# A front that mixes projections with maxima: four copy buffers, six weight-part buffers, rows grouped at the end of the queries, a key row of its own

## The chip, the core and the metric

The kernel runs on one core of a Trainium2 chip. The metric is the device time of one execution in microseconds (us), lower is better. The engines are named as the profile names them: PE (TensorE, matrix multiply), ACT (ScalarE), DVE (VectorE), POOL (GpSimd) and SP (SyncE, which here only issues DMAs). Every engine works through its own list of instructions in order and waits for the others by semaphores; a DMA queue does the same.

## The reference

Two kinds of attention read the same 2048 x 512 input `x`, and a gate mixes them row by row:

```python
x = A_x                                             # 1 x 2048 x 512
g = _sigmoid((x * gate_w).sum(-1, keepdims=True))
a = _A_ref(x, A_wqkv, A_wo)   # 32 heads of 16: each row attends to itself and 7 rows before it, 2 apart
b = _B_ref(x, B_wq, B_wk, B_wv, B_wo)   # 32 query heads, one key head and one value head, full softmax over 2048 rows
return g * a + (1 - g) * b
```

`_A_ref` projects `x @ wqkv` to 1536 columns, `_B_ref` projects 512 columns of queries, 16 of keys and 16 of values. All data are f32. The kernel splits a factor into a high part in the short f32r format and a low part (the rest), and makes a product from three matmuls: high by high, high by low, low by high.

## The kernel before, in words

**Order.** Nothing is scheduled by a tool. The Python code writes the instructions in the order in which it runs, and it decides that order with its own small clock (`clk["pe"]`, `clk["act"]`, `clk["dve"]`, `pool`): whenever a matmul is due, it asks whether a bank is free by that clock, and whether some other piece of work fits beside it. The engines then follow this order, whatever their real times are. Deferred steps lie in a list `tasks` with a due time; `settle(kind, n)` writes out all tasks of a kind but the last `n`.

**Stages.** First a short start (keys, values, first two queries). Then the *front*, `front_stream`: it works through `lumps`, called row parts here: 14 query parts `("q", m)`, then 48 parts `("a", gg, j)` of the projection for branch A, which come in three groups `gg` of 16 (each group is 512 of the 1536 columns, each `j` is 128 rows). Each row part is 12 matmuls on the upper half of the array's rows and 12 on the lower half, and the two halves (two *lines*, `b` = 0 and 1) run side by side. After the front comes the main stage, 512 steps of scores, exponentials and weighted sums for branch B, with POOL working on branch A meanwhile.

**Fours.** The lines take the row parts in fours: line 0 in the order 1st, 3rd, 2nd, 4th and line 1 in the order 2nd, 4th, 1st, 3rd. A row part is thus begun by one line and ended by the other, in the same PSUM bank. The line that comes second may begin only when `may` knows that the first has ended there. There are 62 row parts, so the fourth four holds two query parts and two parts of `gg` 0, and the last group has two row parts.

**Fills.** Between the matmuls of the row parts stand *fills*: scores whose maxima over the keys branch B needs before its exponentials. Early fills are plain: a matmul (line 382) and a DVE maximum (420, 432). Later ones work on halves: max(a, b) = (a+b)/2 + |a-b|/2, where a matmul (481) gives the difference, ACT takes its absolute value (511), another matmul (481) the half sum, and DVE adds both and reduces (529). The half keys come from a matrix `sel`, which `half_sel` builds on DVE from `whole_k` (443 to 449). `whole_k` lies in a buffer with the tag `wkl`, in which every third `qhi` tile (high part of a query, written out by DMA at line 264) lies too.

**Copies of row parts.** When a row part of branch A is done, `a_post` copies its bank to a tile `stage` in SBUF (ACT, line 315) and puts off a task `store`, which writes it by two or three DMAs on SP's queue to `ad` in DRAM (309), in pieces of up to 96 f32 numbers (384 bytes). `stage` has two buffers, so a copy waits until the store of the copy before the last has landed. On ACT everything behind the copy waits too.

**Weights of branch A.** A group has four weight chunks `c` of 128 rows. POOL's queue loads one (`load_wa`, 168) into one of two `waraw` buffers, ACT makes the high part (`split_wa`, recorded at line 119), and POOL makes the low part `wal` a little later (179, a task of the kind `low`). `wah` and `wal` have `WB` buffers each; the first twelve tiles in them are raw parts of `x`. `ahead_wa` loads the next group's chunks at `j` = 2, 4, 6, 8 and splits them at `j` = 5, 7, 9, 11, as many as there are buffers for. Row part `j` uses chunk `c` in its matmuls `i` = 3c to 3c+2, and `may` holds a line back until the low part has been written into the program.

**POOL.** `run_pool` hands POOL the next pieces of branch A while POOL is less than 2.5 us ahead by the kernel's clock; it is not called in the last two row parts of groups 0 and 1.

Of the kernel before, what the change touches and what calls it, by code (L numbers as in the profile page):

```python
# [6 lines left out]
F32 = mybir.dt.float32  # L7
# [6 lines left out]
P = 128  # L14
# [3 lines left out]
DH = 16  # L18
NJ = S // P
C = D // P  # L20
# [13 lines left out]
GG = 3  # L34
GN = NAG * AN // GG
# [9 lines left out]
LEAD, M2S, M1S, E1S, PER_ROW = 3.0, 0.5, 0.3, 0.2, 21  # L45
M2H = 0.15
JUST = 0.05
WB = 8


T_R, T_LAT, T_EXP, T_RED2, T_RED1, T_W, T_TTR = 0.23, 0.20, 0.92, 1.14, 0.61, 1.21, 0.70
# [34 lines left out]
def gated_mix_kernel(ctx, tc, xt, wa, wk, wq, wo_a, wo_b, out):  # L86
# [3 lines left out]
    wp = ctx.enter_context(tc.tile_pool(name="work", bufs=2))  # L90
# [42 lines left out]
    p1 = tc.alloc_tile_pool(name="phase1", bufs=1)  # L133
    p0 = tc.alloc_tile_pool(name="phase0", bufs=1, side="right")
# [7 lines left out]
    wkl = p0.tile([P, C, P], F32R, name="wkl")  # L142
    wqr = [p1.tile([P, 2, C, P], F32, name="wqr", tag="dd", bufs=2) for _ in range(2)]
    waraw, wah, wal = {}, {}, {}

    first = wp.tile([P, 4, 512], F32, name="xraw", tag="aext", bufs=2)
# [23 lines left out]
    def split_wa(gg, c):  # L170
        hi = wah[gg, c] = p1.tile([P, GN], F32R, name="wah", bufs=WB)
        raw = waraw.pop((gg, c))
        high(hi, raw)
        at = after("act", clk["pe"], 0.62)

        def rest():
            nonlocal pool
            wal[gg, c] = p1.tile([P, GN], F32R, name="wal", bufs=WB)
            nc.gpsimd.tensor_sub(wal[gg, c], raw, hi.bitcast(F32))
            pool = max(pool, clk["pe"] * 1e3) + 1300  # L180

        tasks.append((at + 0.3, rest, (), "low"))

    def ahead_wa(gg, k):

        if 0 <= k < 2 * C and k % 2 == 0:
            load_wa(gg, k // 2)
        if 2 < k <= (2 * C if gg == 0 else 2 * (WB - C)) + 1 and k % 2:
            split_wa(gg, (k - 3) // 2)
# [120 lines left out]

    def a_post(gg, j, bank):

        settle("store", 1)
        own = p1.tile([P, GN], F32, name="stage", bufs=2)
        nc.scalar.activation(own, bank, AF.Copy)  # L315
        at = after("act", clk["pe"] + T_LAT, 0.52)

        def store():
            for piece in a_pieces(gg):
                a_store(own, gg, j, *piece)  # L320

        tasks.append((at + 0.5, store, (), "store"))
        if j == NJ - 1:
            tasks.append((at + 1.0, whole, (gg,)))
# [59 lines left out]
    issued, seen, known = [0], {}, [-1]  # L384
# [27 lines left out]
    def fill_pair(dst, key):  # L412
        if dst is m2:
            dst = m2.whole()
        v, pr, t, kc = slots.pop(0)
        m = unit_tile(v)
        mark("m20", "m21")
        for odd in range(2):
            max_mm(dst[:, odd, :], v, pr, t, kc, odd)
        nc.vector.tensor_reduce(m[:, :, pr, t, kc], dst, AX.X, ALU.max)  # L420
        free[key] = after("dve", after("pe", 0, T_R) + T_LAT, T_RED2) + 0.08
        filled(v, 2)
# [16 lines left out]

    def half_sel():  # L440

        whole_k = p0.tile([P, 2, DH], F32, name="wholek", tag="wkl", bufs=1)
        nc.vector.tensor_add(whole_k, twin[:, :, 0, :, 0], twin[:, :, 0, :, 1])
        sel.append(p0.tile([P, 2, P], F32R, name="sel", tag="wkh", bufs=1))
        dd.extend(p1.tile([P, 2, 512], F32, name="dd", bufs=2) for _ in range(2))
        for x in range(2):
            to = sel[0][:, x].rearrange("p (b h z) -> p b h z", b=2, h=2)
            nc.vector.tensor_scalar(to[:, :, 0].rearrange("p b (d s) -> p b d s", s=2), whole_k.unsqueeze(3).to_broadcast([P, 2, DH, 2]), 0.5 - x, 0.0, op0=ALU.mult, op1=ALU.add)
            nc.vector.tensor_scalar(to[:, :, 1].rearrange("p b (s d) -> p b s d", s=2), whole_k.unsqueeze(2).to_broadcast([P, 2, 2, DH]), 0.5 - x, 0.0, op0=ALU.mult, op1=ALU.add)
        after("dve", 0, 1.0)  # L450
# [580 lines left out]
    lumps = []  # L1031
# [18 lines left out]
    def settle(kind, n):  # L1050
        for task in [t for t in tasks if t[3:] == (kind,)][:-n or None]:
            tasks.remove(task)
            task[1](*task[2])
# [141 lines left out]
    def mm(b, at):  # L1195
        nonlocal pool
        x, i = at
        lump = lumps[x]
        if x not in items:
            if lump == ("q", 9):  # L1200
                half_sel()
            elif lump == ("q", 10):
                wants.extend((1, 0))
            items[x] = queries(lump[1]) if lump[0] == "q" else a_project(*lump[1:])
            clk["pe"] = max(clk["pe"], free[f"f{x % 4}"])
            mark(f"f{x % 4}")
        l, r = items[x][i]
        if type(r) is tuple:
            r = r[0][r[1:]]
        h = slice(64 * b, 64 * b + 64)  # L1210
        second = b != x % 2
        nc.tensor.matmul(front_bank(x), l[h], r[h], start=(not second and i == 0), stop=(second and i == 3 * C - 1))  # L1212
        if i == 3 * C - 1:
            ends_at[x] = seen[f"f{x % 4}"] = issued[0]
        issued[0] += 1
        return T_R

    ends_at, posted = {}, set(range(-4, 0))

    def front_bank(x):  # L1220
        return eb[(1, 1, 0, 0)[x % 4]][:, x % 2, :]
# [1 line left out]
    def may(b, x, i):  # L1223
        lump = lumps[x]
        if lump[0] == "a" and (lump[1], i // 3) not in wal:
            return False
        return i > 0 or (x - 4 in posted if b == x % 2 else x in ends_at and known[0] >= ends_at[x])

    def front_stream():

        n, many = 3 * C, len(lumps)
        lines = [[], []]
        for x in range(0, many, 4):
            four = list(range(x, min(x + 4, many)))
            lines[0] += four[0::2] + four[1::2]
            lines[1] += four[1::2] + four[0::2]
        lines = [[(x, i) for x in line for i in range(n)] for line in lines]
        at, idle, begun = [0, 0], 0, False
        while min(at) < n * many:
            lone = {}  # L1240
            if wants and free["m2"] <= clk["pe"] + 0.1:
                half_keys(wants.pop(0))
            halves = groups or any(pend) or paired() and not (half or ended or wants) and free["m2"] <= clk["pe"] + 0.3
            if halves:
                for b in range(2):
                    if sum_ready(b):
                        lone[b] = lambda b=b: fill_sum(b)
                    elif diff_ready(b):
                        lone[b] = lambda b=b: fill_diff(b)
                        break  # L1250
            else:
                for dst, key in ((m1, "m1"), (po, "po")):
                    if not lone and fillable() and free[key] <= clk["pe"] - just():
                        lone[half[0][4] if half else 0] = lambda dst=dst, key=key: fill_one(dst, key)
            moved = []
            for b in sorted((0, 1), key=lambda b: b not in lone):
                if b in lone:
                    now = clk["pe"]
                    lone[b]()
                    clk["pe"] = now  # L1260
                elif at[b] < n * many and may(b, *lines[b][at[b]]):
                    mm(b, lines[b][at[b]])
                    moved.append(lines[b][at[b]])
                    at[b] += 1
            if lone or moved:
                idle = 0
                after("pe", 0, T_R)
            else:
                idle += 1
                assert idle < 400  # L1270
                clk["pe"] += 0.05
                run_tasks()
            if not (ended or wants or halves or formed) and slots and fillable() and free["m2"] <= clk["pe"] - just():
                clk["pe"] = max(clk["pe"], free["m2"])
                fill_pair(m2, "m2")
            if min(at) >= n * many - 9:
                ended.add(1)
            if min(at) >= n * many - 7 and not begun:
                begun = True
                eb[0] = ebs[0].whole()  # L1280
                free["e0"] = max(free["f2"], free["f3"])
                exp_pair(0, 0)
            for x, i in moved:
                if i == n - 1 and counted.count(x):
                    lump_done(x)
                elif i == n - 1:
                    counted.append(x)
            if moved and moved[-1][1] % 3 == 2:
                run_tasks()
                lump = lumps[min(x for x, i in moved)]  # L1290
                if p2 and not (lump[0] == "a" and lump[1] + 1 < GG and lump[2] > NJ - 3):
                    run_pool()
# [61 lines left out]
    for s in range(NS + 1):  # L1354
# [17 lines left out]
        k, n = (outs + rows) // 4 - 1, C - (outs >= NJ - 4)  # L1372
# [19 lines left out]
        first = 0  # L1392
# [3 lines left out]
        while order:  # L1396
            which = order.pop(0)
            if which == "later":
                order[:0] = ["m1", 1] if free["e1"] > clk["pe"] - E1S or bare[0] and free["m1"] < clk["pe"] - 1.0 else [1, "m1"]
                first = 0  # L1400
            elif which == "m2":
                fill_ready("m2", M2S)
            elif which == "m1":
                one = not later_rows and (kt or not s or u >= NU - 8) and singles(s)
                bare[0] = not one
                if one:
                    first = half[0][4] if half else 0
# [95 lines left out]
```

## Time and profile before

| | |
|---|---|
| median of 3 runs | 1464.08 us (1461.46 to 1466.11) |
| the profiled execution, its own time | 1462.15 us |
| its span, first to last instruction | 1460.4 us |
| PE busy | 1435.4 us (98%) |
| ACT / DVE / POOL busy | 1295.5 / 1153.5 / 966.5 us |
| front, first to last matmul of line 1212 | 24.0 to 295 us |

The span is what the trace covers. A window row gives, for a stretch of the span, the busy time of each engine with its number of instructions (x), then the granted PE clock (1.00 is full), the busy share of the DMA engines and the GB/s. A waits row says which engine and line waited for whom: total, times, longest. In a timeline row the bracket at the end is the idle time of that engine just before the instruction, and what ended it.

### The profile page before, as it was taken

What the parts mean: (1) busy time and instruction counts of PE and PEld (TensorE: products, weight loads), DVE (VectorE), ACT (ScalarE), POOL (GpSimd) and SP (SyncE); (2) the same over time, 40 slices, a digit from 0 to 9 for tenths busy, and PEclk for the clock granted to TensorE, in tenths of its full rate; (3) what the DMA queues carried; (4) which work ended last, traced back from release to release, by engine and by line L of the source; (5) the groups of instructions that cost most, each with busy time, mean ns of one, the idle gap of its engine ahead of it and who ended that gap; (6) DMA issues with size and microseconds to landing.
All of it is one profiled execution on the core that took longest, in us unless ns stands there. A gap on an engine that the chain in (4) does not pass through costs nothing.

```text
span 1460.4 us, 29278 instructions
## 1 busy us (share of the span) xinstructions
PE 1435.4 (98%) x10524; PEld 672.6 (46%) x10524; DVE 1153.5 (79%) x1882; ACT 1295.5 (89%) x1645; POOL 966.5 (66%) x1749
## 2 busy tenths in 40 slices
PE   9898999999999999999999999999999999999998
PEld 7676666633333333333333367433333336433343
DVE  8776878878887888888888889788888888788712
ACT  5597878799999999999999988999999998899986
POOL 5451486788898988888889888979888805111121
PEclk9999999999999999999999999999999999999999
DMA  6553433222120210112323110221202010000110
GB/s 226 168 158 99 133 81 115 75 80 63 41 86 14 84 33 30 60 28 75 99 51 98 46 56 31 86 64 44 67 22 72 12 40 28 16 1 2 30 30 30
DMA packets 106970, 94.03 MB, mean 64 GB/s; under 512 B 84880, under 2 KB 89016, under 8 KB 102728
## 3 DMA queue, kind: packets, MB, share of 16 engines
q1 hardware_dynamic: 99864, 52.95, 13.4%
q0 software_dynamic: 6240, 37.89, 7.9%
q8 instruction: 83, 1.36, 0.4%
q10 hardware_dynamic: 720, 1.31, 0.3%
q14 instruction: 63, 0.52, 0.1%
HBM read 62.13 MB, written 29.45 MB: 63 GB/s over the span
## 4 chain that ended last, share of the span: by engine, by line
PE 90%; DMA 2%; issue 2%; ACT 2%; POOL 2%; DVE 2%; SPq 0%; ACTq 0%; POOLq 0%; DVEq 0%
PE po L584 34%; PE pe L574 23%; PE pe L1212 8%; PE pm L382 8%; PE ps L382 5%; PE pe L889 4%; PE pm L481 4%; PE ps L481 2%; PE po L481 1%; DMA ad<-stage 1%; PE pm L943 1%; POOL qst L208 1%; DVE mx L420 1%; ACT dd L511 1%; ACT pexp L576 0%
## 5 line engine op out<-in xcount | busy, mean ns | idle before, releaser
L576 ACT ACTIVATE pexp<-pe 128x1024 f32<-128x1024 f32 x1022 | 983.7, 1023 | 63.9 <-PE pe L574 60.9
L420 DVE TENSOR_REDUCE mx<-pm 128x2 f32<-128x1024 f32 x487 | 595.8, 1223 | 169.1 <-PE pm L382 157.7
L584 PE MATMUL po<-pexp,vst 128*32 128x512 f32 x4096 | 545.5, 605 | 0.4 <-ACT pexp L576 0.4
L574 PE MATMUL pe<-qst,kst 64*128 64x512 f32 x1788 | 419.7, 454 | 1.9 <-ACT pexp L576 1.2
L574 PEld LDWEIGHTS pe<-qst,kst 64*128 64x128 f32 x1788 | 167.5, 183 | 443.5 <-ACT pexp L576 435.7
L432 DVE TENSOR_REDUCE mx<-ps 128x1 f32<-128x512 f32 x309 | 210.3, 681 | 1.7 <-PE ps L382 1.5
L648 POOL TENSOR_TENSOR pr<-aext 128x256 f32<-128x256 f32 x256 | 182.4, 741 | 5.5 <-DMA aext<-ad 5.2
L382 PE MATMUL pm<-kst,qst 62*128 62x512 f32 x913 | 183.4, 397 | 0.4
L711 POOL TENSOR_TENSOR oa<-oa,av 128x256 f32<-128x256 f32 x224 | 164.4, 734 | 15.9
L511 ACT ACTIVATE dd<-pm 128x512 f32<-128x512 f32 x252 | 145.9, 600 | 25.3 <-PE pm L481 6.6
L584 PEld LDWEIGHTS po<-pexp,vst 128*32 128x32 f32 x4096 | 80.6, 108 | 147.1 <-issue 137.0
L708 POOL TENSOR_TENSOR av<-aext,lg 128x256 f32<-128x256 f32 x224 | 139.6, 623 | 12.8
L1212 PE MATMUL pe<-wah,xh 64*128 64x512 f32 x384 | 132.9, 399 | 4.2 <-ACT stage L315 4.2
L1212 PE MATMUL pe<-wal,xh 64*128 64x512 f32 x384 | 131.6, 399 | 0.0
L1212 PE MATMUL pe<-wah,xl 64*128 64x512 f32 x384 | 130.7, 396 | 0.0
L481 PE MATMUL pm<-kcd,qst 62*128 62x512 f32 x286 | 112.7, 404 | 5.6 <-ACT dd L511 5.3
L382 PE MATMUL ps<-kst,qst 62*128 62x512 f32 x291 | 114.8, 395 | 3.2 <-DVE mx L432 3.2
L529 DVE CUSTOM_DVE_ANT_0 dd<-po,dd 128x512 f32<-128x512 f32 x126 | 86.9, 689 | 24.3 <-PE po L481 12.8
L529 DVE CUSTOM_DVE_ANT_0 dd<-ps,dd 128x512 f32<-128x512 f32 x126 | 86.9, 690 | 18.8 <-PE ps L481 7.1
L382 PEld LDWEIGHTS pm<-kst,qst 62*128 62x128 f32 x913 | 87.3, 186 | 3.7 <-DVE mx L420 2.2
L654 POOL TENSOR_TENSOR tr<-pr 128x512 f32<-128x512 f32 x64 | 81.8, 1278 | 4.4
L511 ACT ACTIVATE pexp<-pm 128x512 f32<-128x512 f32 x122 | 68.4, 599 | 15.6 <-PE pm L481 9.0
(205 smaller groups left out, 1957.5 us busy)
## 6 DMA issues: line engine op xcount, KB each, us to landing
aext<-ad POOLq DMA_DIRECT2D x32, 1056.0 KB, 5.6
ad<-stage SPq DMA_DIRECT2D x32, 240.0 KB
qst<-qd SPq DMA_DIRECT2D x56, 128.0 KB
qd<-qhi SPq DMA_DIRECT2D x16, 256.0 KB
qd<-qlo SPq DMA_DIRECT2D x16, 256.0 KB
td<-raw SPq DMA_DIRECT2D x32, 128.0 KB
oa<-td SPq DMA_DIRECT2D x256, 16.0 KB
xraw<-xt SPq DMA_DIRECT2D x15, 256.0 KB
```

Of the source, the lines that this page charges most:

```text
L382: nc.tensor.matmul(dst, qst[home(v)[0]][b:b + 62, pr, t * P:(t + 1) * P], kst[b:b + 62, kc * 512:(kc + 1) * 512], start=True, stop=True)
L420: nc.vector.tensor_reduce(m[:, :, pr, t, kc], dst, AX.X, ALU.max)
L432: nc.vector.tensor_reduce(m[:, odd, pr, t, kc:kc + 1], dst, AX.X, ALU.max)
L481: nc.tensor.matmul(dst, qst[home(v)[0]][b:b + 62, pr, t * P:(t + 1) * P], kcd[b:b + 62, kc // 2, x, :], start=True, stop=True)
L511: nc.scalar.activation(d[:, odd], m2[:, odd, :], AF.Abs)
L529: nc.vector.tensor_tensor_reduce(d[:, odd], dst, d[:, odd], 1.0, -FMAX, ALU.add, ALU.max, m[:, odd, pr, t, kc:kc + 1])
L574: nc.tensor.matmul(bank[:, odd, :], kst[b:b + 64, kt * P:(kt + 1) * P], qst[home(u)[0]][b:b + 64, pr, :], start=True, stop=True)
L576: nc.scalar.activation(e, bank, AF.Exp, scale=SCALE)
L584: nc.tensor.matmul(po[32 * i:32 * i + 32, :], vst[:, kt, :], pexp[s, i // 2][:, i % 2, :], start=(kt == 0), stop=(kt == NJ - 1))
L648: nc.gpsimd.tensor_mul(pr[:, k], q, e[:, o:o + NH, AC:2 * AC])
L711: nc.gpsimd.tensor_add(ao, ao, av)
L1212: nc.tensor.matmul(front_bank(x), l[h], r[h], start=(not second and i == 0), stop=(second and i == 3 * C - 1))
```

## The change

1. `stage` gets four buffers, and `a_post` leaves two stores put off instead of one.
2. `WB` goes from 8 to 6: two pairs of weight parts (`wah`, `wal`) fewer are on chip. `ahead_wa` therefore splits only chunks 0 and 1 of the next group ahead; new code in `front_stream` splits chunks 2 and 3 in the last row part of a group, as soon as both lines are past the chunk whose buffer they take.
3. The fours of the row parts end with the queries: groups of 4, 4, 4, 2 query parts, then twelve fours of branch A. A table `first` says which line begins a row part.
4. `whole_k` gets a place of its own in the pool `wp`.

```diff
-WB = 8
+WB = 6
...
     def a_post(gg, j, bank):
 
-        settle("store", 1)
-        own = p1.tile([P, GN], F32, name="stage", bufs=2)
+        settle("store", 2)
+        own = p1.tile([P, GN], F32, name="stage", bufs=4)
...
-        whole_k = p0.tile([P, 2, DH], F32, name="wholek", tag="wkl", bufs=1)
+        whole_k = wp.tile([P, 2, DH], F32, name="wholek", bufs=1)
...
-        second = b != x % 2
+        second = b != first[x]
...
-        return i > 0 or (x - 4 in posted if b == x % 2 else x in ends_at and known[0] >= ends_at[x])
+        return i > 0 or (x - 4 in posted if b == first[x] else x in ends_at and known[0] >= ends_at[x])
...
-        for x in range(0, many, 4):
-            four = list(range(x, min(x + 4, many)))
+        whole_q = [x for x in range(many) if lumps[x][0] == "q"]
+        for x in list(range(0, len(whole_q), 4)) + list(range(len(whole_q), many, 4)):
+            four = [y for y in range(x, x + 4) if y < many and (lumps[y][0] == lumps[x][0])]
+            first.update({y: k % 2 for k, y in enumerate(four)})
...
+            for gg in range(1, GG):
+                for c in range(WB - C, C):
+                    if (gg, c) not in wah and min(at) >= n * (len(whole_q) + gg * NJ - 1) + 3 * (c - WB + C + 1):
+                        split_wa(gg, c)
```

The number of instructions on each engine stays the same but for a few fills that change their kind. What moves is the order.

PE, the end of the query parts. `pe_94` and `pe_95` are the banks of two row parts, `wqh` and `wql` the parts of the query weights, `wah` and `wal` those of branch A; line 481 is a fill. Before:

```order
L1212 MATMUL pe_95<-xh_116,wql 128x512
L1212 MATMUL pe_94<-xh_116,wql 128x512
L1212 MATMUL pe_90<-wah,xh 128x512
L1212 MATMUL pe_89<-wah,xh 128x512
L1212 MATMUL pe_90<-wal,xh 128x512
L481 MATMUL ps<-kcd,qst_77 128x512
L1212 MATMUL pe_90<-wah,xl 128x512
L481 MATMUL pm<-kcd,qst_78 128x512
```

After:

```order
L1212 MATMUL pe_95<-xh_116,wql 128x512
L1212 MATMUL pe_94<-xh_116,wql 128x512
L481 MATMUL ps<-kcd,qst_77 128x512
L481 MATMUL pm<-kcd,qst_78 128x512
L481 MATMUL po<-kcd,qst_77 128x512
L481 MATMUL pm<-kcd,qst_78 128x512
L481 MATMUL ps<-kcd,qst_78 128x512
L1212 MATMUL pe_94<-xh_115,wqh 128x512
```

The last two query parts now change lines with five fills and no row part between; branch A's first matmuls come after all queries.

ACT, copies of row parts (line 315) and high parts of weights (119). Before, early in group 0, at the place where the trace shows the longest wait of a copy:

```order
L315 ACTIVATE stage<-pe_94 128x512
L339 ACTIVATE gate_t<-gate 32x16
L511 ACTIVATE dd<-pm 128x512
L315 ACTIVATE stage<-pe_95 128x512
L119 ACTIVATE wah<-waraw 128x512
L511 ACTIVATE dd<-pm 128x512 x2
L339 ACTIVATE gate_t<-gate 32x16
L315 ACTIVATE stage<-pe_89 128x512
L511 ACTIVATE dd<-pm 128x512
L315 ACTIVATE stage<-pe_90 128x512
L119 ACTIVATE wah<-waraw 128x512
```

After, at the border of groups 0 and 1:

```order
L315 ACTIVATE stage<-pe_89 128x512
L511 ACTIVATE dd<-pm 128x512
L315 ACTIVATE stage<-pe_90 128x512
L511 ACTIVATE dd<-pm 128x512
L119 ACTIVATE wah<-waraw 128x512
L511 ACTIVATE dd<-pm 128x512
L119 ACTIVATE wah<-waraw 128x512
L511 ACTIVATE dd<-pm 128x512
L315 ACTIVATE stage<-pe_94 128x512
L511 ACTIVATE dd<-pm 128x512
L315 ACTIVATE stage<-pe_95 128x512
```

Four copies still come close together; the two late high parts stand between the second and the third of them.

POOL, the low parts (line 179) at the border of groups 1 and 2, among pieces of branch A (698 to 711). After:

```order
L698 TENSOR_TENSOR asum<-asum,gate 128x16
L699 TENSOR_TENSOR lg<-lg,asum 128x128
L708 TENSOR_TENSOR oa<-aext,lg 128x8x32
L708 TENSOR_TENSOR av<-aext,lg 128x256
L711 TENSOR_TENSOR oa<-oa,av 128x8x32
L708 TENSOR_TENSOR av<-aext,lg 128x256
L179 TENSOR_TENSOR wal<-waraw,wah 128x512 x2
L711 TENSOR_TENSOR oa<-oa,av 128x8x32
```

Before, the last low part of group 2 stood in an earlier piece of branch A, alone:

```order
L708 TENSOR_TENSOR av<-aext,lg 128x256
L711 TENSOR_TENSOR oa<-oa,av 128x8x32
L179 TENSOR_TENSOR wal<-waraw,wah 128x512
L708 TENSOR_TENSOR av<-aext,lg 128x256
L711 TENSOR_TENSOR oa<-oa,av 128x8x32
L637 DMA aext<-ad 128x2112
L690 TENSOR_TENSOR half<-lg 128x64
```

Two low parts have moved from there to the border, one behind the other. At the border of groups 0 and 1 the two stand just ahead of POOL's first load of rows from `ad` (line 637):

```order
L179 TENSOR_TENSOR wal<-waraw,wah 128x512
L168 DMA waraw<-wa 128x512
L546 TENSOR_TENSOR mt<-mt,mk 128x32
L547 TENSOR_TENSOR ml<-mt,mh 128x32
L179 TENSOR_TENSOR wal<-waraw,wah 128x512 x2
L637 DMA aext<-ad 128x2112 x2
```

More of the change, by code (lines that the diff above doesn't have):

```diff
@@ L1216, in mm @@
         return T_R
-    ends_at, posted = {}, set(range(-4, 0))
+    ends_at, posted, first = {}, set(range(-4, 0)), {}
     def front_bank(x):
```

## The prediction

> **What bounds the kernel now.** I read the page first, then windows of the main stage, then the waits of PE from the start of the front to its end.
>
> ```profile
> PE 1435.4 (98%) x10524; PEld 672.6 (46%) x10524; DVE 1153.5 (79%) x1882; ACT 1295.5 (89%) x1645; POOL 966.5 (66%) x1749
> ...
> 400.00:600.00 200.00, 199.98 (x1434) 73.90 (x1426) 163.92 (x194) 189.66 (x205) 173.45 (x333) 1.00 0.16 51
> ...
> PE pm L481 <- ACT dd L511: 6.2, 10, 2.4
> PE pe L1212 <- ACT stage L315: 4.2, 1, 4.2
> PE ps L382 <- DVE mx L432: 3.2, 1, 3.2
> PE pe L1212 <- ACT qhi L278: 2.0, 1, 2.0
> ```
>
> The main stage is full: in 200 us PE pauses for 0.02 us. It works through a fixed list, so a microsecond gained in the front ends the kernel a microsecond earlier. Nearly all of PE's idle time is in the front, in four rows. Only the front can therefore pay for this change, and the question is which of these four waits it takes away and which it adds.
>
> **The key row of its own.** The third wait begins on DVE.
>
> ```profile
> DVE wholek L443 <- DMA qd<-qhi: 4.2, 1, 4.2
> ...
> ACT wah L119 <- DMA waraw<-wa: 3.1, 1, 3.1
> ...
> 47.20 0.19 DVE L443 TENSOR_TENSOR wholek<-ident 128x32 f32<-128x32 f32 x1 [4.20 <-DMA qd<-qhi]
> ...
> 48.59 0.49 PE L382 MATMUL ps<-kst,qst 62*128 62x512 f32 x1 [3.20 <-DVE mx L432]
> ```
>
> The tiny addition into `whole_k` waits 4.20 us for the store of a query part that used its buffer before. The maximum (432) behind it on DVE frees the bank that the fill at 48.59 needs, so PE stands for 3.20 us. With a place of its own the addition depends only on a constant. The wait goes entirely: 3.2 us. At best DVE's whole 4.2; at worst 2.0, because the next chain (ACT's 3.1 us for a weight load, line 119, ahead of the 2.0 of line 278) is not touched and could come nearer. I take 3.2.
>
> **Four buffers for the copies.** This is the wait of 4.16 us and part of the first row.
>
> ```profile
> ACT stage L315 <- DMA ad<-stage: 12.3, 6, 5.2
> ...
> 119.77 0.60 SPq L351 DMA_DIRECT2D held<-qd  x1
> ...
> 122.34 0.95 SPq L309 DMA_DIRECT2D ad<-stage  x2
> ...
> 127.62 0.60 ACT L315 ACTIVATE stage<-pe 128x512 f32<-128x512 f32 x1 [5.22 <-DMA ad<-stage]
> ...
> 128.28 0.49 PE L1212 MATMUL pe<-wah,xh 64*128 64x512 f32 x1 [4.16 <-ACT stage L315]
> ...
> 124.20:128.30 4.10, 0.03 (x2) 0.03 (x2) 0.00 (x0) 0.65 (x2) 0.00 (x0) 1.00 0.55 146
> ...
> 128.30:130.00 1.70, 1.70 (x8) 1.05 (x10) 0.61 (x1) 1.68 (x4) 1.03 (x1) 0.66 0.44 121
> 130.00:132.00 2.00, 2.00 (x12) 1.84 (x11) 0.70 (x4) 1.19 (x3) 0.24 (x1) 0.50 0.15 32
> 132.00:134.00 2.00, 2.00 (x18) 1.81 (x17) 1.73 (x5) 1.57 (x4) 0.00 (x0) 0.94 0.00 0
> 134.00:136.00 2.00, 2.00 (x20) 1.49 (x20) 1.91 (x7) 1.77 (x4) 0.00 (x0) 1.00 0.00 0
> ```
>
> The store two copies back stood on SP's queue behind four loads of stacked queries (119.77 on), was issued at 122.34 and landed some 5 us later. ACT waited 5.22 us for it, with the differences of the fills (511) and a high part (119) queued behind, and PE 4.16 us. Then the granted clock is 0.66 and 0.50. A full window of 2 us has 20 matmuls; 128.30 to 134.00 has 8 + 12 + 18 = 38 where 57 would stand, and 19 at 10 per us are 1.9 us. Together 4.2 + 1.9 = 6.1 us. The bounds: 4.2 if the clock falls at some other wait instead, 6.5 with 0.4 us for uncertain edges of the windows.
>
> The Trainium skill explains the second half ("TensorE: Matmul & The Clock Gate", Part 1: an idle window of about 3.4 us halves the array's clock, and a busy one restores it). The trace agrees: 3.20 us idle left it at 1.00, 4.16 us did not. By the rule one cold window of 3.4 us costs an estimated 1.7 us, so the sum would move by 0.2; but the windows run freely, so waits near 3 us may be dearer in one run than in another.
>
> With four buffers a copy waits for the store four copies back. The copies come four at a time, and the four of the next round stand behind a dozen and more differences on ACT (0.6 us each, 7 us and more) besides their own four row parts. A store that lands 5 us after its issue is in time.
>
> The other five waits of ACT sum to 12.3 - 5.2 = 7.1 us. What they cost PE:
>
> ```profile
> 181.81 0.49 PE L481 MATMUL pm<-kcd,qst 62*128 62x512 f32 x1 [2.45 <-ACT dd L511]
> ...
> 214.61 0.50 PE L481 MATMUL pm<-kcd,qst 62*128 62x512 f32 x1 [0.62 <-ACT dd L511]
> 216.74 0.49 PE L481 MATMUL pm<-kcd,qst 62*128 62x512 f32 x1 [0.70 <-ACT dd L511]
> ...
> 160.00:170.00 10.00, 10.00 (x88) 7.25 (x86) 8.71 (x26) 8.58 (x18) 4.12 (x7) 1.00 0.86 271
> 170.00:220.00 50.00, 44.71 (x368) 32.03 (x368) 38.01 (x114) 38.59 (x74) 41.53 (x80) 1.00 0.37 95
> 220.00:240.00 20.00, 19.95 (x168) 14.17 (x164) 17.74 (x54) 17.23 (x33) 10.66 (x19) 1.00 0.31 87
> 240.00:290.00 50.00, 49.04 (x383) 33.20 (x380) 42.54 (x127) 40.29 (x78) 38.73 (x80) 1.00 0.31 87
> 290.00:296.00 6.00, 5.31 (x40) 3.54 (x38) 5.01 (x16) 4.64 (x8) 5.45 (x9) 1.00 0.53 186
> ```
>
> Three pauses, 2.45 + 0.62 + 0.70 = 3.8 us, with some slower matmuls around them: 368 in 50 us. At the rate of the next 20 us (168) there would be 420, and 52 at 8.8 per us are 5.9 us. At the rate of the later 50 us, where a copy hardly waits but POOL and DVE have branch A as here, there would be 383, and 15 are 1.7 us. Bounds 1.7 and 5.9; I take 4.0, next to the 3.8 that is really idle.
>
> **Two weight pairs fewer.** No instruction goes; chunks 2 and 3 of groups 1 and 2 are split about 41 matmuls before they are used. That count: per line 15 of the row parts' matmuls lie between, two lines, and 2033 matmuls of the front's order for 1474 of line 1212. At 88 in 10 us it is 4.7 us. In this time ACT must make two high parts and POOL two low parts:
>
> ```profile
> 180.65 0.62 ACT L119 ACTIVATE wah<-waraw 128x512 fp32r<-128x512 f32 x1
> ...
> 212.92 1.29 POOL L179 TENSOR_TENSOR wal<-waraw,wah 128x512 fp32r<-128x512 f32 x1
> ...
> 160.57 1.11 POOL L637 DMA_DIRECT2D aext<-ad  x2 [16.96 <-DMA qst<-ml]
> ```
>
> 0.62 + 1.29 + 1.29 = 3.2 us. At the first border POOL has nothing else, so it fits, less an ACT queue of one or two differences of 0.6. At the second, POOL can be 2.5 us ahead with branch A, and its pieces stand in front: 3.2 + 1.2 + 2.5 = 6.9 against 4.7, plus 0.9 us since the second chunk is needed later than the first. That is 1.3 us of PE waiting; with 0.2 for the first border I take +1.5. Bounds: nothing, and both borders without any cover, 2 x 3.2 = 6.4.
>
> **Fours that end with the queries.** Before, the pair of two row parts that changes lines with nothing between stood at the end of the front: 40 matmuls in 290 to 296, where 88 per 10 us make 53; 13 are 1.5 us, part of it the switch to the main stage. Now it stands at the end of the queries with five fills to fill it. I take 0, between 1.5 lost and 1.5 gained. Branch A's rows come later in the order, hence POOL's first load of rows too, but POOL idles 16.96 us before that load, and its busy tenths in 40 slices of the span fall to one or two for the last sixth:
>
> ```profile
> POOL 5451486788898988888889888979888805111121
> ```
>
> **Fills.** The order has 3 more fill matmuls in the front and 3 fewer behind; at 1434 per 200 us these are 0.4 us off the main stage, which I count as -0.4 (0 to -0.8).
>
> **Sum.** -3.2 - 6.1 - 4.0 + 1.5 + 0 - 0.4 = -12.2. From the profiled execution's own 1462.15 (span 1460.4 and 1.75 around it) that gives 1450.0. The median of the runs, 1464.08, lies 1.9 above that execution, so I forecast 1452.0 as a median.
>
> **The rivals.**
>
> *The gain is given back to ACT and DVE.* During the long pause both drained their queues, and the stretch behind it ran full. Without the pause, 128 to 160 may run as 240 to 290 does (383 in 50 us, 77 per 10 us against 88): 34 matmuls less in 30 us, 3.9 us; and 170 to 220 gives only 1.7. Sum: -3.2 - 6.1 + 3.9 - 1.7 + 1.5 - 0.4 = -6.0, so 1458. For it speak ACT and DVE busy for 8 to 9 of 10 us throughout; against it, 90 to 124 ran near full with no pause ahead.
>
> ```profile
> 90.00:124.20 34.20, 34.03 (x289) 25.25 (x285) 28.50 (x84) 29.69 (x62) 12.81 (x16) 1.00 0.52 146
> ```
>
> *The stores are short of bandwidth, not of buffers.* Then four buffers only put the wait off by two copies; what stays is -3.2 - 0.4 + 1.5 = -2.1: 1462. The DMA share of 0.52 to 0.55 around the wait speaks against it. The Trainium skill speaks for it ("DMA: Bandwidth & Descriptors", Specifications: pieces under 512 bytes do not reach the full rate), and most packets here are of that kind:
>
> ```profile
> DMA packets 106970, 94.03 MB, mean 64 GB/s; under 512 B 84880, under 2 KB 89016, under 8 KB 102728
> ```
>
> *The late low parts wait behind POOL's own wait.* If the two low parts at the first border were caught behind the load that waited 16.96 us, PE would stand that long and lose 1.9 more to the clock: -13.7 + 17.0 + 1.9 = +5.2, so 1469, slower. This side begins where the borders cost more than 13.7 us. The order speaks against it: the low parts stand ahead of that load.
>
> *The key row does nothing.* If DVE's addition is held by something else than the buffer (its place in the order is the same), 3.2 us stay: 1455.
>
> **How the numbers follow.** Forecast 0.62, given back 0.19, key row 0.08, bandwidth 0.05, late low parts 0.05, others 0.01. The best ends together give -4.2 - 6.5 - 5.9 + 0 - 1.5 - 0.8 = -18.9, 1445; the worst without a rival -2.0 - 4.2 - 1.7 + 6.4 + 1.5 = 0.0, 1464. Few terms will lie at the same end, so the range is 1445 to 1460, with the first and last rival reaching to its upper part. A measurement of this kernel tells a difference of 0.3%, 4.4 us. Below 1459.7 lie the forecast, the key row and over half of the first rival: 0.81. Within lie the rest of these and the bandwidth: 0.14. Slower: 0.05.
>
> **What would show it.** Right: `whole_k` without a wait, `stage` without a wait for `ad`, no clock below 1.00 between 30 and 280 us, line 574 beginning 10 to 13 us earlier, waits of PE or its weight loads for `wal` of one or two us at the second border only. Wrong: a wait of line 1212 for 179 or 119 of over 3.2 us at a border, ACT's copies still waiting for `ad`, or more of line 481 waiting for 511 than the 6.2 us now.

## The result, and the profile after

The changed kernel takes 1446.47 us, the median of four runs (1444.96 to 1447.14), against 1464.59 (1461.46 to 1466.11) for the kernel before in the same comparison: a ratio of 0.9878 with a 95% interval of 0.9859 to 0.9896, or 18.1 us less. The forecast was 1452.0 and 12.2 us less. The spans of the two profiled executions, 1460.4 and 1443.0, differ by 17.4 us.

The busy line of the engines, from the page of the kernel after, answers to the first line shown of before:

```profile
PE 1432.9 (99%) x10524; PEld 675.9 (47%) x10524; DVE 1152.0 (80%) x1883; ACT 1297.3 (90%) x1649; POOL 963.9 (67%) x1749
```

The work is the same. PE's busy time went down by 2.5 us, near the 1.9 us that the prediction gave to the low clock. The rest was idle time, and it went from the front. These are the waits of PE in the kernel after, from 24 to 300 us: who waits for whom, total, times, longest.

```profile
PE pe L1212 <- ACT qhi L278: 1.8, 1, 1.8
PE pe L574 <- ACT stage L315: 0.9, 1, 0.9
PE pe L574 <- ACT pexp L576: 0.5, 1, 0.5
```

Of the four rows of before only the wait of 2.0 us for line 278, which the change does not touch, is left. The waits for 511, for the copy (315) and for the maximum (432) are gone. Among ACT's waits of the same time there is no row `stage <- ad` any more, where 12.3 us stood.

To see where the time came from, I count matmuls from a common start. Each row below starts at 24 us and ends later than the one above; the first number with an x is the count of matmuls that PE had done by then. First before, then after.

```profile
24.00:124.00 100.00, 94.68 (x779) 75.21 (x778) 79.47 (x178) 68.78 (x158) 43.15 (x44) 1.00 0.51 146
...
24.00:140.00 116.00, 106.52 (x864) 84.41 (x865) 88.27 (x205) 79.11 (x180) 44.43 (x45) 0.99 0.47 134
...
24.00:170.00 146.00, 136.41 (x1116) 106.07 (x1117) 114.09 (x280) 105.51 (x230) 50.30 (x55) 0.99 0.48 136
...
24.00:220.00 196.00, 181.12 (x1482) 138.10 (x1483) 152.10 (x394) 144.11 (x303) 91.83 (x134) 0.99 0.45 126
...
24.00:270.00 246.00, 230.68 (x1870) 171.40 (x1871) 195.02 (x520) 185.66 (x381) 127.89 (x206) 0.99 0.42 118
```

```profile
24.00:124.00 100.00, 97.94 (x806) 80.04 (x806) 83.94 (x191) 73.79 (x168) 43.29 (x44) 1.00 0.54 152
...
24.00:140.00 116.00, 113.94 (x940) 91.72 (x940) 98.25 (x233) 88.67 (x197) 43.77 (x46) 1.00 0.50 140
...
24.00:170.00 146.00, 143.94 (x1196) 114.26 (x1196) 125.55 (x313) 114.96 (x247) 63.68 (x81) 1.00 0.50 143
...
24.00:220.00 196.00, 193.80 (x1604) 150.38 (x1604) 168.59 (x441) 157.73 (x329) 103.26 (x154) 1.00 0.47 133
...
24.00:270.00 246.00, 243.72 (x2004) 185.05 (x2002) 211.67 (x569) 199.41 (x408) 144.61 (x237) 1.00 0.45 128
```

The lead of the kernel after is 27 matmuls at 124 us, 76 at 140, 80 at 170, 122 at 220 and 134 at 270. The rate of a stretch of the kernel after is its own count over its length (806 in 100 us, 134 in 16, 256 in 30, 408 in 50, 400 in 50), so the gains are 3.3 us up to 124 (where the wait for the key row stood), 5.8 between 124 and 140 (where the long wait and its low clock stood), 0.5 up to 170, 5.1 between 170 and 220, and 1.5 up to 270. That is 16.2 us. The last matmul of line 1212 starts at 278.2 us instead of 294.6, which is 16.4 us earlier, and the stretch behind it is 1.0 us shorter. Both together are the 17.4 us of the spans.

The low parts of the weights, which the change makes late, stand in time on POOL. These are rows of POOL's timeline in the kernel after, at the first border of groups and at the second:

```profile
141.69 2.55 POOL L179 TENSOR_TENSOR wal<-waraw,wah 128x512 fp32r<-128x512 f32 x2 [9.08 <-ACT wah L119]
...
147.34 1.11 POOL L637 DMA_DIRECT2D aext<-ad  x2 [3.10 <-DMA ad<-stage]
...
208.64 2.56 POOL L179 TENSOR_TENSOR wal<-waraw,wah 128x512 fp32r<-128x512 f32 x2 [0.38 <-ACT wah L119]
```

At the first border POOL was free (9.08 us idle ahead of the pair), and the load that could have blocked it stands behind. At the second the pair begins 0.38 us after ACT's high part. PE waits for neither.

### The profile page after: what moved, and what is told of

It is laid out like the page before. It is cut to its first block, busy times and chain, and to the rows that moved or that the text cites. A ratio compares the mean times of both kernels' runs of the same rounds, so it can differ in the third digit from the quotient of the medians.

```text
span 1443.0 us, 29289 instructions
## 1 busy us (share of the span) xinstructions
PE 1432.9 (99%) x10524; PEld 675.9 (47%) x10524; DVE 1152.0 (80%) x1883; ACT 1297.3 (90%) x1649; POOL 963.9 (67%) x1749
## 4 chain that ended last, share of the span: by engine, by line
PE 97%; DMA 1%; ACT 1%; DVE 1%; issue 0%; SPq 0%; POOL 0%; ACTq 0%; POOLq 0%; DVEq 0%
PE po L584 35%; PE pe L574 24%; PE pe L1212 11%; PE pm L382 8%; PE ps L382 5%; PE pe L889 4%; PE pm L481 4%; PE ps L481 2%; PE po L481 2%; PE pm L943 1%; DMA qd<-qhi 0%; ACT pexp L576 0%; PE pe L238 0%; DMA waraw<-wa 0%; PE po L204 0%
## 5 line engine op out<-in xcount | busy, mean ns | idle before, releaser
L432 DVE TENSOR_REDUCE mx<-ps 128x1 f32<-128x512 f32 x303 | 206.2, 681 | 2.6 <-PE ps L382 2.5
L1212 PE MATMUL pe<-wah,xh 64*128 64x512 f32 x384 | 129.4, 395 | 0.0
L611 POOL TENSOR_TENSOR rl<-rl,gate_t 128x16 f32<-128x16 f32 x31 | 6.9, 222 | 115.3 <-DVE rl L605 76.0
```

Of the source, the lines that this page charges most:

```text
L432: nc.vector.tensor_reduce(m[:, odd, pr, t, kc:kc + 1], dst, AX.X, ALU.max)
```

## The experiments

The trace of after shows which waits went, but not which of the four parts took them away. Eleven kernels were run, each timed in five rounds beside the kernel before (medians 1463.74 to 1465.01). The theory was that of the prediction: two buffers are too few, four take away the waits of the copies, and the key row is a separate gain. The first rival was that the parts do less than their waits (gain given back, bandwidth, key row without effect); a later one, that the order of the row parts and not the buffers did it.

**The key row alone, and the change without it.** First the kernel before with only this edit:

```diff
-        whole_k = p0.tile([P, 2, DH], F32, name="wholek", tag="wkl", bufs=1)
+        whole_k = wp.tile([P, 2, DH], F32, name="wholek", bufs=1)
```

> The kernel before with only the key row in a place of its own. Theory (each wait that is removed pays by itself): the addition into whole_k no longer waits, PE's 3.20 us at 48.6 us are gone, 3 us faster than before, about 1461.5. Rival (the next chain moves nearer): the 2.0 us wait for line 278 grows and less than 1.5 us remain. The rival by which the key row does nothing: the time of before.

It took 1459.52 us, 5.1 less than before, ratio 0.9969 (0.9958 to 0.9980). The wait for 432 is gone and the wait of 4.2 us for the copy is still there. Between the two profiled executions the gain is only 2.2 us (spans of 1460.4 and 1458.2). The other way round, the changed kernel with the line removed above put back:

> The changed kernel with whole_k back in the buffer it shared. Theory (the parts add up): 3 us slower than the changed kernel, about 1449.5, with PE idle 3 us near 48 us. Rival (the wait is hidden once the rest flows): the time of the changed kernel within 1 us.

It took 1451.48 us, 5.0 more than the changed kernel, ratio to before 0.9922 (0.9905 to 0.9939). Both are more than the 3.2 us that PE stood idle. A reason shows on PE in this second kernel, one row of its timeline and then four windows from 48 us on:

```profile
48.39 0.49 PE L382 MATMUL ps<-kst,qst 62*128 62x512 f32 x1 [2.20 <-DVE mx L432]
```

```profile
48.00:50.00 2.00, 1.61 (x12) 1.35 (x14) 2.00 (x4) 0.00 (x0) 0.00 (x0) 0.89 0.76 224
50.00:52.00 2.00, 2.00 (x12) 1.54 (x12) 2.00 (x4) 0.00 (x0) 0.00 (x0) 0.50 0.20 70
52.00:54.00 2.00, 2.00 (x17) 1.63 (x15) 1.11 (x3) 0.68 (x2) 0.00 (x0) 0.75 0.00 0
...
62.00:64.00 2.00, 0.58 (x2) 0.50 (x4) 0.03 (x1) 2.00 (x5) 1.53 (x2) 0.81 0.88 269
```

Behind a pause of only 2.20 us the granted clock is 0.50 and then 0.75, with 29 matmuls in 4 us where 40 would stand: 1.1 us more. The profiled execution of before had the full clock here after 3.20 us. A second fall follows in the same execution, behind the wait of 2.11 us for line 278: 0.81 in the last row, then 0.50 from 64 to 66 us. The kernel after kept 1.00 behind its wait of 1.83 us there. Behind that wait PE goes on at 63.42 instead of 58.79, 4.6 us late, and the first copies of row parts come 6.2 us late (97.61 against 91.45), near the 6.7 us by which the two spans differ (1449.7 and 1443.0).

So the same wait costs more in some executions than in the one that I read, and a median holds these too. The executions on record point the same way: the kernel before had a mean granted clock of 0.994 to 0.998 in this comparison, the five slowest with 0.994 or 0.995, and with the key row alone it was 0.996 to 0.999. The execution of before that I read had 0.999. This explains the direction of the excess; that it explains all of the 1.8 us was not shown.

**The buffers back to two.** The changed kernel with the old buffering:

```diff
-        settle("store", 2)
-        own = p1.tile([P, GN], F32, name="stage", bufs=4)
+        settle("store", 1)
+        own = p1.tile([P, GN], F32, name="stage", bufs=2)
```

> The changed kernel with two stage buffers and one store put off, as before. Theory (the buffers carry most): ACT waits for ad again, some 12 us in all, the long pause of PE with the low clock comes back; 11 to 14 us slower than the changed kernel, about 1459. Rival (the new order of the fours carries the part that the forecast lacked, 5 us): only 5 to 8 us slower, about 1453, with the waits for ad smaller than the 12.3 us of before.

1457.02 us, 10.5 more than the changed kernel, ratio 0.9953 (0.9939 to 0.9967). The size is about that of the two copy terms of the prediction, but not the place. No long wait came back in the middle of the front. One of PE's waits, one row of PE's timeline, one of ACT's, and two of PE's windows:

```profile
PE pe L574 <- ACT stage L315: 5.3, 1, 5.3
...
288.49 1.22 PE L574 MATMUL pe<-qst,kst 64*128 64x512 f32 x4 [5.28 <-ACT stage L315]
...
287.84 0.60 ACT L315 ACTIVATE stage<-pe 128x512 f32<-128x512 f32 x1 [4.30 <-DMA ad<-stage]
...
290.00:292.00 2.00, 2.00 (x9) 0.49 (x10) 1.82 (x2) 2.00 (x3) 0.00 (x0) 0.50 0.39 103
...
294.00:296.00 2.00, 2.00 (x12) 0.20 (x8) 1.23 (x1) 1.83 (x2) 0.00 (x0) 0.50 0.57 200
```

The wait is now at the very end of the front: the last four row parts are copied within 10 us, the fourth copy waits 4.30 us for the store of the second, and the main stage (574) waits 5.28 us for the bank of that copy. Behind it the clock stays at 0.50 up to 296. This is not the whole loss: the first of these four copies is already 4.4 us later than in the changed kernel (278.71 against 274.32).

**The same with all eight weight pairs.** As the last, and `WB = 8`, so that no part is split late. Against the kernel before it has the key row and the fours alone.

> As the run with two buffers, but with eight weight pairs, so that all chunks are split ahead. Against that run it prices the late splits. Theory (hidden): same time within 1 us. Rival (the late splits cost the forecast 1.5 us): 1 to 3 us faster than the run with two buffers and six pairs.

1449.15 us, ratio 0.9900 (0.9884 to 0.9916): 15.4 us of the 18.1 without a single buffer more. The wait at the end of the front is there, but shorter:

```profile
PE pe L574 <- ACT stage L315: 2.7, 1, 2.7
```

With two buffers the late splits thus cost 7.9 us (1457.02 against 1449.15). Most of it does not lie in the wait at the end. The windows from 220 to 270, first with six pairs, then with eight:

```profile
220.00:270.00 50.00, 48.21 (x388) 33.56 (x386) 41.39 (x125) 40.89 (x78) 40.38 (x83) 1.00 0.33 89
```

```profile
220.00:270.00 50.00, 49.82 (x418) 35.78 (x414) 44.69 (x134) 42.59 (x82) 40.03 (x82) 1.00 0.37 105
```

PE falls behind by 30 matmuls here, and by 50 from 120 to 270, which is 6 us at 8.4 per us, without a pause of 1 us or more and at a clock of 1.00. Why the late splits slow the groups so with two buffers is not settled.

**Seven pairs with four buffers.** `WB = 7` in the changed kernel, so one chunk of a group is split late instead of two.

> The changed kernel with seven weight pairs instead of six: one late chunk per border. Theory (late splits are hidden): same time within 1 us. Rival (they cost): 1 to 2 us faster than the changed kernel.

1445.36 us (1443.76 to 1446.87), ratio 0.9876 (0.9857 to 0.9895), against 0.9878 for six pairs. With four buffers the second late chunk of a group thus costs 1.1 us by the medians, which these intervals do not tell from nothing. Four buffers with eight pairs, and four buffers with the old fours, were not tried. So what the late splits cost as a whole with four buffers, and what more buffers do for the old fours, is not shown.

**Three buffers.** `bufs=3` in the changed kernel:

> The changed kernel with three stage buffers. Theory (a store lands some 5 us after its issue and four copies come close together): the third and fourth copy of a round still wait a little, 0 to 3 us slower than with four. Rival (one more buffer than two is all that was lacking): the same time, no wait of ACT for ad. By the bandwidth rival the waits would be nearly those of two buffers, 8 us and more slower.

1446.46 us, ratio 0.9881 (0.9863 to 0.9899): the same as with four, and no copy waits for `ad`. One buffer more than before was enough. If the stores had been short of bandwidth, three buffers would have brought part of the waits back.

**The fours alone.** Since two buffers gave 15.4 us together with the fours and the key row, the fours had to carry much of it. The kernel before with part 3 of the change only: the new groups and the table `first`; eight pairs, two buffers and the shared `whole_k` stay.

```diff
-        second = b != x % 2
+        second = b != first[x]
...
-        for x in range(0, many, 4):
-            four = list(range(x, min(x + 4, many)))
+        whole_q = [x for x in range(many) if lumps[x][0] == "q"]
+        for x in list(range(0, len(whole_q), 4)) + list(range(len(whole_q), many, 4)):
+            four = [y for y in range(x, x + 4) if y < many and (lumps[y][0] == lumps[x][0])]
+            first.update({y: k % 2 for k, y in enumerate(four)})
```

> The kernel before with only the fours that end with the queries (eight pairs, two buffers, shared buffer for whole_k). Theory (the fours only make the late splits possible): before within 2 us. Rival (the fours carry the 5 us that the forecast lacked, by copies that come at better moments): 4 to 6 us faster than before, about 1459.5, and ACT waits for ad less than 12.3 us.

1453.76 us, 10.4 less than before, ratio 0.9935 (0.9919 to 0.9951). The step that the prediction took as 0 is the largest. Waits of PE and of ACT, two windows (the first of them for 120 to 140, where before had 120 matmuls), and the new pause at the end of the front with a window behind it:

```profile
PE pe L574 <- ACT stage L315: 2.6, 1, 2.6
...
ACT stage L315 <- DMA ad<-stage: 4.7, 4, 1.6
...
120.00:140.00 20.00, 19.88 (x170) 14.70 (x168) 16.09 (x49) 18.36 (x40) 4.90 (x6) 1.00 0.45 118
170.00:220.00 50.00, 49.03 (x410) 35.41 (x408) 41.75 (x125) 42.13 (x81) 41.61 (x81) 1.00 0.39 106
...
285.85 1.22 PE L574 MATMUL pe<-qst,kst 64*128 64x512 f32 x4 [2.63 <-ACT stage L315]
...
288.00:290.00 2.00, 2.00 (x10) 0.30 (x10) 1.35 (x2) 1.68 (x2) 1.84 (x3) 0.50 0.94 309
```

With two buffers still, the copies wait 4.7 us instead of 12.3, and both slow stretches run nearly full. Why is seen on SP's queue. Here are a copy (315), the stores (309) and the loads of stacked queries (351) around it, from the timelines of ACT and of SP in the kernel with the fours alone:

```profile
114.13 2.06 SPq L309 DMA_DIRECT2D ad<-stage  x4
116.24 0.54 SPq L351 DMA_DIRECT2D held<-qd  x1
...
119.49 0.95 SPq L309 DMA_DIRECT2D ad<-stage  x2
...
114.47 0.61 ACT L315 ACTIVATE stage<-pe 128x512 f32<-128x512 f32 x1
...
118.81 0.59 ACT L315 ACTIVATE stage<-pe 128x512 f32<-128x512 f32 x1
```

These are row parts `j` = 4 to 7 of `gg` 0, one four. The stores of 4 and 5 go out together (114.13, x4), and loads follow. The copy of 7, at 118.81, needs the buffer of 5, whose store was issued by 116.2, and it does not wait.

In the kernel before, two row parts of `gg` 0 share a four with the last queries, so the fours are 2 to 5 and 6 to 9. Loads are written behind the copies of `j` = 2, 4, 6, 8. The long wait is at 6 to 9, and the program has there, in this order:

```
before:      copy 6, loads, copy 7, store 6, copy 8, loads, store 7, copy 9
fours alone: copy 6, loads, copy 7, store 6, store 7, copy 8, loads, copy 9, store 8
```

A store is written when it is due or when the next copies force it. Before, 7 and 8 lie in one four, 2.5 us apart on ACT (118.82 and 121.32), and the loads of `j` = 8 come before store 7 is due. Copy 9 needs the buffer of copy 7 and waits. With the new fours 8 begins another four, its copy comes 10.7 us after that of 7 (129.46 against 118.81), and both stores are out by then.

**The reading tested from the other side.** Without moving row parts: in the kernel before, all stores that are put off are written ahead of the loads.

```diff
             if gg == 0 and j in (2, 4, 6, 8):
+                settle("store", 0)
                 stack(len(stacked))
```

> The kernel before, with all put-off stores written out ahead of each stack's four loads in group 0, so that on SP's queue no stack stands between the stores of two copies of a four. Nothing else changes. Theory (the long wait of 5.22 us at 122 us is the place of the stack on SP's queue, which the new fours moved): that wait falls under 2 us, PE's pause of 4.16 us and the low clock behind it go, 4 to 6 us faster than before, about 1459. Rival (the fours help by the spacing of the copies, and any second store of a four is late): ACT's waits for ad stay near 12 us and the time stays within 1.5 us of before.

1470.88 us, 5.9 more than before, ratio 1.0042 (1.0027 to 1.0056). A miss: I had expected a gain. The edit writes the store of the row part just copied ahead of the loads. On SP's queue the loads now wait until that copy is made, and the store of the next row part stands behind them. SP's queue and ACT's timeline of this kernel:

```profile
102.17 0.94 SPq L309 DMA_DIRECT2D ad<-stage  x2
103.22 0.62 SPq L351 DMA_DIRECT2D kept<-qd  x1
...
107.27 2.14 SPq L309 DMA_DIRECT2D ad<-stage  x4
...
102.50 0.62 ACT L315 ACTIVATE stage<-pe 128x512 f32<-128x512 f32 x1
...
111.74 0.60 ACT L315 ACTIVATE stage<-pe 128x512 f32<-128x512 f32 x1 [4.14 <-DMA ad<-stage]
```

The store of the copy at 102.50 (`j` = 3) goes out only at 107.27, behind the loads and two further DMAs (line 562), and the copy of `j` = 5, two later, waits 4.14 us for it. The same happens once more at 133.57, with 4.80 us. The loads between two stores make the wait, here in the direction that I had not wanted. So the loads were moved by one row part as well, to stand behind pairs:

```diff
-            if gg == 0 and j in (2, 4, 6, 8):
+            if gg == 0 and j in (3, 5, 7, 9):
+                settle("store", 0)
                 stack(len(stacked))
```

> The kernel before, with each stack of group 0 issued one row part later and all put-off stores written out ahead of it, so that the stores stand in pairs and a stack's four loads only between pairs (the run with the stores first had put a stack between the two stores of a pair twice, and had two waits of 4 to 5 us). Theory (a stack between the first and the second store of a four makes the fourth copy wait): the wait of 5.22 us and PE's pause of 4.16 us with its low clock go, 4 to 6 us faster than before, about 1459. Rival (the fours act by the spacing of the copies): some copy of group 0 still waits 4 us or more, and the time is that of before or above.

1458.77 us, 5.0 less than before, ratio 0.9965 (0.9956 to 0.9975). A wait of PE, two windows, and a copy in ACT's timeline:

```profile
PE pm L481 <- ACT dd L511: 4.7, 12, 1.7
...
120.00:140.00 20.00, 19.92 (x172) 14.99 (x170) 16.54 (x50) 18.45 (x38) 3.13 (x3) 1.00 0.45 118
...
170.00:220.00 50.00, 46.59 (x382) 33.42 (x382) 39.68 (x119) 39.80 (x76) 39.99 (x79) 1.00 0.41 108
...
177.87 0.60 ACT L315 ACTIVATE stage<-pe 128x512 f32<-128x512 f32 x1 [2.24 <-PE pe L1212]
```

The long wait and its low clock are gone with two buffers, eight pairs and the old fours: 172 matmuls between 120 and 140. So that wait was one of order on a queue. The stretch from 170 to 220 is still slow (382 against 410 with the new fours). The copy at 177.87 is put down to PE, but it stands where before a copy waited 3.01 us for `ad`, the fourth of its four; a wait for several semaphores goes to the one that came last by the profile. Why the new fours make the copies of this group wait less (at most 1.42 us there, with the fours alone) is not settled.

**Two versions beyond the change.** What is left of PE's waits is the 1.8 us for 278, which follows on ACT's 2.9 us for the second weight chunk of group 0. Both chunks loaded at the same place in the changed kernel:

```diff
-        if 0 <= k < 2 * C and k % 2 == 0:
+        if 0 <= k < 2 * C and k % 2 == 0 and (gg or k != 2):
             load_wa(gg, k // 2)
+            if not gg and not k:
+                load_wa(gg, 1)
```

> The changed kernel with the second weight chunk of group 0 loaded together with the first, so that ACT does not wait 2.9 us for it near 55 us. Theory (each wait that PE shows in the front is worth its length): PE's 1.83 us at 58.8 us go, 1 to 2 us faster than the changed kernel, about 1445. Rival (the earlier load only delays the stores of query parts beside it): no change or up to 1 us slower.

1442.90 us (1442.33 to 1445.03), ratio to before 0.9862 (0.9844 to 0.9880), 3.6 us below the changed kernel by the medians. Both waits are gone. The windows from 24 to 60, first of the changed kernel, then of this one:

```profile
24.00:60.00 36.00, 34.02 (x278) 31.55 (x278) 31.58 (x45) 20.19 (x57) 18.02 (x16) 1.00 0.57 163
```

```profile
24.00:60.00 36.00, 36.00 (x293) 29.98 (x292) 33.21 (x48) 20.12 (x58) 18.93 (x17) 1.00 0.57 165
```

PE is busy for all 36 us. The interval overlaps that of the changed kernel, whose ratio comes from another comparison, so this is the fastest by median and probably faster, by an amount that is not settled. With seven pairs as well:

> The changed kernel with seven weight pairs and the second weight chunk loaded early, the two variants that came out at or below the changed kernel, together. Theory (they act at different places and add up): about 1442, 1 us below the early load alone. Rival (each only shifts the order, and the sum is within the noise of the early load alone, or above it): 1443 to 1444.

1443.34 us, ratio 0.9851 (0.9836 to 0.9866): not told apart from the last. The two do not add up to anything that could be measured.

## Why the prediction was right, and where its steps were wrong

Right were the direction, the place and the way to the end: the waits of the front went, the main stage passed on all of the gain, and 1446.5 lies in the range. It lies near the lower end, since the sum was 5.9 us short. That it lies within at all is in part luck: the change holds the buffers and the new fours, so waits that the prediction put down to the wrong part went all the same. Of the signs, no wait of `whole_k` or for `ad` and a clock of 1.00 came true; line 574 began 16.5 us earlier (276.0 instead of 292.5) and not 10 to 13, and no wait for `wal` came at the second border. Step by step:

| step | forecast | trace or run |
|---|---|---|
| key row | -3.2 | -3.3 by counts; -5.1 alone, 5.0 lost without it |
| long wait of a copy and low clock | -6.1 | -5.8 by counts |
| other waits of copies | -4.0 | -0.5 (140 to 170), -5.1 (170 to 220) and -1.5 (220 to 270) by counts |
| late weight splits | +1.5 | no wait of PE; with four buffers 1.1 or nothing for one chunk of the two, with two buffers 7.9 |
| fours that end with the queries | 0 | -10.4 alone |
| fills | -0.4 | -1.0 behind the front, not shown to be the fills |

- **Four buffers for the copies.** The waits were the right ones and their sizes near. The cause was at best half of it. The prediction quoted the loads at 119.77 ahead of the store at 122.34 and still put the wait down to the number of buffers. The runs with the fours alone and with the loads behind pairs remove that wait with two buffers. Whether more buffers would have removed it with the old fours was not tried.
- **Fours that end with the queries** is the step that failed. I looked only at the pair of row parts that it moves, and not at what else hangs on a row part's number: the loads at `j` = 2, 4, 6, 8 get another place within a four, and so among the stores on SP's queue.
- **The parts overlap.** In a chain the medians give -10.4 for the fours, -5.0 for the key row on top (1449.15 with another comparison's median before), and -2.7 for buffers and six pairs together. The buffers alone look larger, 10.5 us when undone, since with two buffers the fours and the late splits make a wait of 2.6 to 5.3 us at the end of the front, and the late splits slow the groups ahead of it; with a third buffer both are gone. The sum of the prediction had no such term, and its terms for copies, right in size, stood under the wrong part.
- **Late weight splits**: the wait of 1.3 us at the second border did not come, since the queue of POOL that I had added was not there (0.38 us idle ahead of the pair).
- **The key row** was read from one execution in which the clock held. A term for a wait behind which the clock falls in some executions is larger in a median.
- **The four rows** were said to be nearly all of PE's idle time. They are 15.6 of 25.0 us; 17.0 lie in the front. The sum did not rest on this.

The rivals: *given back to ACT and DVE* is refuted, as the kernel after is ahead by another 4 matmuls between 140 and 170 and does not fall back later. *Bandwidth* is refuted by three buffers. The Trainium skill ("DMA: Bandwidth & Descriptors", Specifications) holds that pieces under 512 bytes do not reach the full rate; here the stores have pieces of at most 384 bytes, and with three buffers no copy waited for them, so that rule did not set the time. *Late low parts behind POOL's own wait* is refuted by POOL's rows at 141.69 and 147.34. *The key row does nothing* is refuted by both of its runs.

## What to carry to other kernels

Before a wait for a store is answered with more buffers, look at what stands between the copy and the issue of its store on the queue: here four loads between two stores were the long wait, and moving them needed no memory. When a step renumbers or regroups work, follow everything that is triggered by those numbers, on every queue, since the largest effect can come from an instruction that the step does not name. And parts that ease the same wait do not add up: measure each alone and each removed, and expect the next late place, here the last four copies ahead of the main stage.

## What the runs showed of the chip that was not expected

The granted clock does not follow the length of a pause alone. It fell to 0.50 after 2.20 us of idle PE (key row undone) and after 2.63 (fours alone, end of the front), and held at 1.00 after 3.20 (kernel before). The Trainium skill ("TensorE: Matmul & The Clock Gate", Part 1) says that an idle window of about 3.4 us is needed, and that the windows run freely; the second half would make equal pauses cost differently, as seen here, but a drop after 2.20 us is below that figure, and the measurement decides. How long the low clock lasts differs as well, and it seems to come in steps. If a clock between 0.50 and 1.00 in a window is read as a mix of the two, the low time is 3.4 us behind the wait of 4.16 us (kernel before) and behind the one of 2.20 us (key row undone). It is 6.8 us behind the 2.63 us of the fours alone (0.88 from 284 to 286, 0.50 to 292, 0.92 to 294). It is 10.2 us behind the 5.28 us with two buffers (0.63 from 286 to 288, 0.50 to 296, 0.81 to 298). These are one, two and three times 3.4 us. What decides between them is not shown.
